# One transposition for the token numbers of each expert, and a later one for the scales

## The chip, the cores and the metric

The kernel runs on one core of a Trainium2 chip. The metric is the device time of one execution in microseconds (us); the times below are those of whole executions, and the profile is of one execution more. The engines are TensorE (PE, with its weight loads as PEld), VectorE (DVE), ScalarE (ACT), GpSimd (POOL) and SyncE (SP), whose queue here issues most transfers. Each engine works through its instructions in the order in which the program lists them.

## What is computed

A gated linear recurrence gives one row of 384 numbers to each of 3072 tokens. A router then picks one of 8 experts for each token, and a second network follows:

```python
logits = x @ w_gate
e_idx = np.argmax(logits, axis=1)
...
gate_w = probs[np.arange(N), e_idx]
eom = 1.0 / (1.0 + np.exp(-(x @ w_output_gate)))
...
    h = np.maximum(x[mask] @ w1[e], 0.0)
    ye = h @ w2[e]
    out[mask] = gate_w[mask, None] * eom[mask, e, None] * ye
...
h = np.maximum(np.maximum(x @ w1, x @ w2), x @ w3)
return (h @ w_out)
```

The factor `gate_w * eom` is one positive number for a token, its scale. The second network lets it through, so the kernel multiplies by it at the very end.

## The kernel before

The recurrence comes first (function `attention`). It writes each token's row with an indirect transfer into the part of the DRAM array `xs` that belongs to its expert. A row there has 385 columns: 384 numbers and, in the last, the token's own number. The experts are ranked by how many tokens they got, and rank e has room for `CAPS[e]` tokens (480, 444, 428, 412, 400, 392, 380, 372).

Then come the experts (function `experts`), 8 of 8 steps each, numbered s = 8e + f. In a step TensorE executes `up(e, f)`, one block of nine matmuls of 128 hidden units for all tokens of the expert (tile `php`), and `down` of the step before, nine matmuls that add into three accumulators (`pacc`). Each product is made of three matmuls (lines 715 to 717) over numbers split in a high and a low part. After `up`, ScalarE makes the high part `hh` (L731) and VectorE the low part `hl` (L732), which the next step's `down` reads. At the last step of an expert the accumulators are copied into `yT` (L746 on ScalarE, L748 on VectorE).

What else a step does is in a table: `at(s, f, ...)` lists a function under a step, and `step(s)` calls the functions of that step after the matmuls, in the order in which they were listed. This order is written out by hand for every engine (`tc.manual_schedule(engines=None)`), so nothing overtakes. The functions that matter here:

- `load_x(e + 1)` in step 8e + 1 fetches the next expert's tokens into `xe`, of which there is one buffer. `transpose_x(e + 1)` in step 8e + 4 turns them (TensorE, `pxt`) and splits them (`xh`, `xl`).
- `numbers(e)` in step 8e (step 1 for e = 0) takes the last column of `xe`, the tokens' numbers, and turns it into lines. TensorE transposes the equal blocks together and the shorter rest by itself, both into the PSUM tile `pid`, and VectorE copies each out (`lines`, `rest`).
- `offset(e)` in step 8e + 5 writes the lines to `ids_d` in DRAM, at a place that a register holds: a transfer for `lines`, and one for `rest`.
- `gates` in step 6 computes all scales on VectorE and ScalarE (`sc`), transposes them on TensorE (`psc`), copies them (`sr`) and sends them to `scale_d` from GpSimd's queue.
- `divide(n)` splits a weight array: `wh` on ScalarE (L156), `wl` mostly on GpSimd (L159). `narrow` (L651 to L653) and `finish` (L659, L660) convert the second network's weights in steps 4j + 2 and 4j + 3.

PSUM has four buffers for `php`, `pxt`, `pid` and `psc` together, taken in turn, and four for `pacc`.

The last stage works through the tokens in the order of `ids_d`: it loads those numbers (L875), fetches the scales by them, and scatters the rows of the result.

Of the kernel before, what the change touches and what calls it, by code (L numbers as in the profile page):

```python
# [10 lines left out]
F32 = mybir.dt.float32  # L11
# [9 lines left out]
B, H, S, D = 4, 8, 768, 48  # L21
HD = H * D
C = 128
NC = S // C
# [4 lines left out]
CAPS = [480, 444, 428, 412, 400, 392, 380, 372]  # L29
# [123 lines left out]
def split(nc, hi, lo, src, hi_eng=None, lo_eng=None):  # L153

    if hi_eng is None:
        nc.scalar.copy(hi, src)  # L156
    else:
        hi_eng.tensor_copy(hi, src)
    (lo_eng or nc.vector).tensor_tensor(out=lo, in0=src, in1=hi.bitcast(F32), op=ALU.subtract)  # L159
# [427 lines left out]
def experts(ctx, tc, io, xs, R, ids_d, scale_d, V32):  # L587

    nc = tc.nc
# [4 lines left out]
    kp = ctx.enter_context(tc.tile_pool(name="kp", bufs=1))  # L594
    yT = kp.tile([128, 3, TP], F32, name="yT")
    LEAST = [e * NT // E for e in range(E)]
    idn = R["idn"]
# [65 lines left out]
        n, i, view = NARROW[j]  # L663
        nc.sync.dma_start(view(V32[n], i), single.pop(j)[0])

    X, RAWX = {}, {}

    def places_of(e):

        if e == 0:  # L670
            n = CAPS[0] // 4
            return [(r * n, n, n) for r in range(4)]
        last = CAPS[e] - 384
        return [(r * 128, 128, min(128, CAPS[e] - r * 128)) for r in range(3)] + ([(384, last, last)] if last > 0 else [])

    def load_x(e):
# [9 lines left out]
                (nc.scalar if k == 1 else nc.sync).dma_start(x[:n, :, ks], src[:, ks].rearrange("(r p) n -> p r n", r=4))  # L686
        X[e] = x

    def numbers(e):

        p = pq.tile([128, 512], F32, tag="pq", name="pid")
        blocks = places_of(e)
        same = [b for b in blocks if b[2] == blocks[0][2]]
        n = same[0][2]
        t = [kp.tile([4, 128], F32, tag="lines", name="lines", bufs=1), kp.tile([1, 128], F32, tag="rest", name="rest", bufs=1)]
        lines = [(0, len(same), n)] + [(len(same) + i, 1, m) for i, (_, _, m) in enumerate(blocks[len(same):])]
        for i, (r, k, m) in enumerate(lines):
            nc.tensor.transpose(p[:k, i * 128:i * 128 + m], RAWX[e][:m, r:r + k, HD], idn[:m, :m])
            nc.vector.tensor_copy(t[i][:k, :m], p[:k, i * 128:i * 128 + m])
        R["lines", e] = t, [(blocks[r][0], k, m) for r, k, m in lines]  # L700

    def transpose_x(e):
        n = CAPS[e]
        hi = xp.tile([128, 3, CAP], F32R, tag="xh", name="xh")[:, :, :n]
        lo = xp.tile([128, 3, CAP], F32R, tag="xl", name="xl")[:, :, :n]
        for k in range(3):
            p = pq.tile([128, 512], F32, tag="pq", name="pxt")
            for r, (r0, _, m) in enumerate(places_of(e)):
                nc.tensor.transpose(p[:, r0:r0 + m], X[e][:m, r, k * 128:(k + 1) * 128], idn[:m, :m])  # L709
            split(nc, hi[:, k], lo[:, k], p[:, :n])  # L710
        RAWX[e], X[e] = X[e], (hi, lo)

    def three(out, st_, mv, start, stop):
        (sh, sl), (mh, ml) = st_, mv
# [50 lines left out]
    def offset(e):  # L765
        R["off"][e] = nc.values_load(R["oi"][0:1, e:e + 1], engines=[ENG.DVE, ENG.Activation, ENG.SP], min_val=LEAST[e], max_val=min(NT, sum(CAPS[:e])),
                                     skip_runtime_bounds_check_because="a sum of counts")
        to = ids_d[bass.ds(R["off"][e], CAPS[e])]
        t, lines = R["lines", e]
        for i, (r0, k, m) in enumerate(lines):  # L770
            nc.sync.dma_start(to[r0:r0 + k * m].rearrange("(r p) o -> r (p o)", r=k), t[i][:k, :m])

    def gates():

        T = B * NC
        lg, oh = R["lg"], R["oh"]
        dl = lg
        nc.vector.tensor_tensor(out=dl[:, :, :E], in0=lg[:, :, :E], in1=R["mx"].unsqueeze(2).to_broadcast([128, T, E]), op=ALU.subtract)
        nc.vector.tensor_tensor(out=dl[:, :, E:], in0=lg[:, :, E:], in1=oh, op=ALU.mult)
        s2 = kp.tile([128, 2, T], F32, name="s2")  # L780
        nc.scalar.activation(out=dl[:, :, :E], in_=dl[:, :, :E], func=AF.Exp)
        nc.vector.tensor_reduce(out=s2[:, 1], in_=dl[:, :, E:], axis=AX.X, op=ALU.add)
        nc.scalar.activation(out=s2[:, 1], in_=s2[:, 1], func=AF.Exp, scale=-1.0)
        nc.vector.tensor_reduce(out=s2[:, 0], in_=dl[:, :, :E], axis=AX.X, op=ALU.add)
        nc.vector.tensor_scalar(out=s2[:, 1], in0=s2[:, 1], scalar1=1.0, scalar2=None, op0=ALU.add)
        nc.vector.scalar_tensor_tensor(out=s2[:, 0], in0=s2[:, 0], scalar=1e-9, in1=s2[:, 1], op0=ALU.add, op1=ALU.mult)
        sc = kp.tile([128, T], F32, name="sc")
        nc.vector.reciprocal(sc, s2[:, 0])
        p = pq.tile([128, 512], F32, tag="pq", name="psc")
        nc.tensor.transpose(p[:T, :128], sc, idn)  # L790
        sr = kp.tile([T, 128], F32, name="sr")
        nc.vector.tensor_copy(sr, p[:T, :128])
        nc.gpsimd.dma_start(scale_d.rearrange("(t p) o -> t (p o)", p=128), sr)
# [4 lines left out]
    def at(s, f, *args):  # L798
        todo.setdefault(max(s, 0), []).append(lambda: f(*args))
# [23 lines left out]
    divide(0, nc.vector)  # L823
    keep_warm(nc, pq.tile([128, 512], F32, tag="pq", name="idle"), idn.bitcast(BF16), WARM[1])
    transpose_x(0)
    divide(1, nc.gpsimd)
    for n in range(2, N1 + N2):
        s = n - 3 if n < N1 else N1 - 19 + (n - N1) * 3 // 2
        at(s, divide, n, nc.vector if n == 2 or n > N1 and n % 2 else nc.gpsimd)
        if n >= 4:  # L830
            at(s - 3, bring, n)
    at(3, offsets)
    at(6, gates)
    for k in range(3):
        at(4 + 3 * k, nc.gpsimd.memset, yT[:, k, CAP:], 0.0)
    for e in range(E):
        at(8 * e or 1, numbers, e)
        at(8 * e + 5, offset, e)
        if e + 1 < E:
            at(8 * e + 1, load_x, e + 1)  # L840
            at(8 * e + 4, transpose_x, e + 1)
# [312 lines left out]
def build(ctx, tc, io):  # L1154
# [26 lines left out]
    for e in range(E):  # L1181
        nc.gpsimd.memset(R["ec"][:, 0, e:e + 1], float(e))
    attention(tc, io["a"], io["qk"], io["v"], io, xs, R)
    experts(tc, io, xs, R, ids_d, scale_d, V32)
    flag = nc.values_load(R["flag"][0:1, 0:1], min_val=0, max_val=128, skip_runtime_bounds_check_because="a count of partitions")
    with tc.If(flag > 0):
# [71 lines left out]
```

## Time and profile before

| | |
|---|---|
| time, median of 3 executions | 831.02 us (830.90 to 832.41) |
| profiled execution | 836.34 us, of which the span from first to last instruction is 834.6 us |
| TensorE matmuls busy | 794.7 us, 95% of the span |
| TensorE weight loads busy | 711.3 us, 85% |
| VectorE busy | 475.8 us, 57% |
| ScalarE busy | 385.6 us, 46% |
| GpSimd busy | 272.5 us, 33% |
| mean granted clock of TensorE | 0.98 |

Matmuls are pipelined, so the start of one to the start of the next is what one costs, not its listed duration. The granted clock is the share of full speed that TensorE got in a stretch: it has two levels, 2.4 GHz (1.00) and 1.2 GHz (0.50), and a value between is a mean of both. A wait is idle time of an engine ahead of an instruction, with the instruction that ended it.

### The profile page before, as it was taken

To read this page: it belongs to the slowest core of one execution; us is meant where nothing else is said; L and a number is where in the kernel's file an instruction comes from. 1 tells how busy PE (TensorE), PEld (TensorE's weight loads), DVE (VectorE), ACT (ScalarE), POOL (GpSimd) and SP (SyncE) were. 2 spreads that over 40 slices of the span, in tenths; PEclk is the share of its full clock that TensorE was granted. 3 is DMA by queue.
4 is the path that set the end of the run, shared out by engine and by line. 5 is a ranking of instruction groups with operands and counts; after the bars stand their busy time and mean duration, and the time that the engine had idled before them with its cause. 6 is when DMAs were issued, how large, how long until landed. Compare 5 with 4: busy or idle time off the path is not lost.

```text
span 834.6 us, 13739 instructions
## 1 busy us (share of the span) xinstructions
PE 794.7 (95%) x5164; PEld 711.3 (85%) x5164; DVE 475.8 (57%) x931; ACT 385.6 (46%) x640; POOL 272.5 (33%) x254
## 2 busy tenths in 40 slices
PE   8889999999996989999999899999999999999995
PEld 6678888888895878898999899888888888888995
DVE  3679998998753555576576643334334343334531
ACT  7779999997641434344444454221212112111221
POOL 1022323323222457445455576031211313021301
PEclk9989999999998999999999899999999999999998
DMA  8974425322213746556656665002012021020200
GB/s 273 269 208 156 159 79 174 112 83 84 83 55 84 260 133 226 185 170 199 224 178 208 208 211 170 1 1 75 20 57 95 1 95 33 26 95 0 96 20 22
DMA packets 61633, 100.78 MB, mean 121 GB/s; under 512 B 7138, under 2 KB 44921, under 8 KB 60537
## 3 DMA queue, kind: packets, MB, share of 16 engines
q1 hardware_dynamic: 57162, 90.11, 34.5%
q0 software_dynamic: 3904, 9.49, 3.1%
q8 instruction: 42, 0.69, 0.4%
q10 hardware_dynamic: 495, 0.25, 0.1%
q14 instruction: 30, 0.25, 0.1%
HBM read 79.64 MB, written 20.15 MB: 120 GB/s over the span
## 4 chain that ended last, share of the span: by engine, by line
PE 55%; DVE 6%; issue 5%; ACT 1%; POOL 1%; DMA 1%; SPq 0%; DVEq 0%; POOLq 0%; ACTq 0%
PE pqt L716 8%; PE pqt L717 8%; PE pqt L715 8%; PE php L715 4%; PE php L716 4%; PE php L717 4%; PE pacc L716 3%; PE pacc L715 3%; PE pacc L717 3%; PE pot L717 3%; PE pot L715 3%; PE pot L716 3%; PE pxt L709 2%; DVE w L653 1%; DVE w L660 1%
## 5 line engine op out<-in xcount | busy, mean ns | idle before, releaser
L159 POOL TENSOR_TENSOR wl<-wraw,wh 128x768 fp32r<-128x768 f32 x68 | 132.8, 1959 | 112.0 <-ACT wh L156 81.1
L717 PE MATMUL pqt<-gh,wl 128*128 128x512 f32 (+1 forms) x378 | 136.1, 360 | 0.0
L716 PE MATMUL pqt<-gl,wh 128*128 128x512 f32 (+1 forms) x378 | 136.0, 360 | 0.0
L715 PE MATMUL pqt<-gh,wh 128*128 128x512 f32 (+1 forms) x378 | 135.7, 359 | 0.0
L156 ACT CAST hh<-h 128x512 fp32r<-128x512 f32 (+1 forms) x42 | 23.5, 560 | 151.2 <-DVE h L905 151.2
L904 DVE TENSOR_TENSOR h<-h,pqt 128x512 f32<-128x512 f32 (+1 forms) x42 | 25.7, 612 | 110.6 <-PE pqt L717 110.6
L731 ACT ACTIVATE hh<-php 128x480 fp32r<-128x480 f32 (+7 forms) x64 | 33.1, 516 | 118.7 <-PE php L717 118.7
L732 DVE SCALAR_TENSOR_TENSOR hl<-php,hh 128x480 fp32r<-128x480 f32 (+7 forms) x64 | 37.4, 584 | 80.3 <-ACT hh L731 80.3
L717 PEld LDWEIGHTS pqt<-gh,wl 128*128 128x128 f32 x378 | 71.3, 189 | 10.6
L716 PEld LDWEIGHTS pqt<-gl,wh 128*128 128x128 f32 x378 | 71.3, 189 | 10.0
L715 PEld LDWEIGHTS pqt<-gh,wh 128*128 128x128 f32 x378 | 71.3, 189 | 9.9
L715 PE MATMUL php<-xh,wh 128*128 128x480 f32 (+7 forms) x192 | 70.2, 366 | 0.0
L716 PE MATMUL php<-xl,wh 128*128 128x480 f32 (+7 forms) x192 | 68.7, 358 | 0.0
L717 PE MATMUL php<-xh,wl 128*128 128x480 f32 (+7 forms) x192 | 68.5, 357 | 0.0
L715 PE MATMUL pacc<-hh,wh 128*128 128x480 f32 (+7 forms) x192 | 67.7, 352 | 0.0
L716 PE MATMUL pacc<-hl,wh 128*128 128x480 f32 (+7 forms) x192 | 67.6, 352 | 0.0
L717 PE MATMUL pacc<-hh,wl 128*128 128x480 f32 (+7 forms) x192 | 67.5, 351 | 0.0
L509 POOL TENSOR_TENSOR run<-run,oh 128x8 bf16<-128x8 bf16 x24 | 13.5, 565 | 161.8 <-DVE oh L486 128.5
L156 ACT CAST wh<-wraw 128x768 fp32r<-128x768 f32 x76 | 61.8, 828 | 9.7 <-DMA wraw<-w 9.3
L903 ACT COPY h<-pqt 128x512 f32<-128x512 f32 (+1 forms) x42 | 22.1, 526 | 88.2 <-PE pqt L717 88.2
L931 POOL DMA_INDIRECT out<-orow,ic x24 | 24.0, 1001 | 117.0 <-ACT orow L930 111.9
L411 PE MATMUL pt<-qT,kT 96*128 96x128 f32 x384 | 51.9, 281 | 2.1 <-DVE qT L212 2.1
(165 smaller groups left out, 1808.8 us busy)
## 6 DMA issues: line engine op xcount, KB each, us to landing
wraw<-w SPq DMA_DIRECT2D x64, 384.0 KB
fa<-a SPq DMA_DIRECT2D x8, 1152.0 KB
a<-a SPq DMA_DIRECT2D x11, 768.0 KB
qk<-qk SPq DMA_DIRECT2D x11, 768.0 KB
raw<-v SPq DMA_DIRECT2D x9, 768.0 KB
xs<-fill SPq DMA_DIRECT2D x8, 721.9 KB
v<-v SPq DMA_DIRECT2D x11, 512.0 KB
xe<-xs SPq DMA_DIRECT2D x21, 192.5 KB
```

The source lines that it names most:

```text
L156: nc.scalar.copy(hi, src)
L159: (lo_eng or nc.vector).tensor_tensor(out=lo, in0=src, in1=hi.bitcast(F32), op=ALU.subtract)
L411: eng.matmul(p[:, z * 128:(z + 1) * 128], lhsT=d["kT", j][:, h], rhs=d["qT", j][:, h], start=True, stop=True)
L709: nc.tensor.transpose(p[:, r0:r0 + m], X[e][:m, r, k * 128:(k + 1) * 128], idn[:m, :m])
L715: nc.tensor.matmul(out, lhsT=sh, rhs=mh, start=start, stop=False)
L716: nc.tensor.matmul(out, lhsT=sh, rhs=ml, start=False, stop=False)
L717: nc.tensor.matmul(out, lhsT=sl, rhs=mh, start=False, stop=stop)
L731: nc.scalar.activation(out=hi, in_=p, func=AF.Relu)
L732: nc.vector.scalar_tensor_tensor(out=lo, in0=p, scalar=0.0, in1=hi.bitcast(F32), op0=ALU.max, op1=ALU.subtract)
L903: nc.scalar.copy(h, pp[0])
L904: nc.vector.tensor_tensor(out=h, in0=h, in1=pp[1], op=ALU.max)
L931: i = nc.gpsimd.indirect_dma_start(out=io["out"], out_offset=bass.IndirectOffsetOnAxis(ap=R["ic", n][:, :1], axis=0), in_=o, in_offset=Non ...
```

## The change

The numbers no longer go through TensorE from `xe`. `numbers(e)` is called at the end of `transpose_x(e)`, and copies the last column of each block of `xe` into a column of a small tile `ln` (128 x 4) on GpSimd. A new function `turn(e)` in step 8e + 2 transposes `ln` as a whole and copies it to `lines`. `offset(e)` writes four lines of equal length in one transfer; what lies beyond an expert's tokens in it is written over by the next expert's. `gates` ends with the reciprocal, and its transposition, copy and transfer are a new function `scales` in step 11.

```diff
-    X, RAWX = {}, {}
+    X = {}
...
+    ln = kp.tile([128, 4], F32, name="ln")
+    lines = kp.tile([4, 128], F32, name="lines")
+    nc.vector.memset(ln, float(1 << 20))
+
     def numbers(e):
 
+        blocks = places_of(e)
+        for r, (_, n, _) in enumerate(blocks):
+            nc.gpsimd.tensor_copy(ln[:n, r:r + 1], X[e][:n, r, HD:])
+
+    def turn(e):
+
         p = pq.tile([128, 512], F32, tag="pq", name="pid")
-        blocks = places_of(e)
-        same = [b for b in blocks if b[2] == blocks[0][2]]
-        n = same[0][2]
-        t = [kp.tile([4, 128], F32, tag="lines", name="lines", bufs=1), kp.tile([1, 128], F32, tag="rest", name="rest", bufs=1)]
-        lines = [(0, len(same), n)] + [(len(same) + i, 1, m) for i, (_, _, m) in enumerate(blocks[len(same):])]
-        for i, (r, k, m) in enumerate(lines):
-            nc.tensor.transpose(p[:k, i * 128:i * 128 + m], RAWX[e][:m, r:r + k, HD], idn[:m, :m])
-            nc.vector.tensor_copy(t[i][:k, :m], p[:k, i * 128:i * 128 + m])
-        R["lines", e] = t, [(blocks[r][0], k, m) for r, k, m in lines]
+        nc.tensor.transpose(p[:4, :128], ln, idn)
+        nc.vector.tensor_copy(lines, p[:4, :128])
...
-        RAWX[e], X[e] = X[e], (hi, lo)
+        numbers(e)
+        X[e] = (hi, lo)
...
-        to = ids_d[bass.ds(R["off"][e], CAPS[e])]
-        t, lines = R["lines", e]
-        for i, (r0, k, m) in enumerate(lines):
-            nc.sync.dma_start(to[r0:r0 + k * m].rearrange("(r p) o -> r (p o)", r=k), t[i][:k, :m])
+        n = places_of(e)[0][1]
+        nc.sync.dma_start(ids_d[bass.ds(R["off"][e], 4 * n)].rearrange("(r p) o -> r (p o)", r=4), lines[:, :n])
...
         nc.vector.reciprocal(sc, s2[:, 0])
+        R["sc"] = sc
+
+    def scales():
+        T = B * NC
         p = pq.tile([128, 512], F32, tag="pq", name="psc")
-        nc.tensor.transpose(p[:T, :128], sc, idn)
+        nc.tensor.transpose(p[:T, :128], R["sc"], idn)
...
+    at(11, scales)
...
-        at(8 * e or 1, numbers, e)
+        at(8 * e + 2, turn, e)
```

On VectorE, the stretch from expert 0's last block to the fourth block of expert 1 (steps 7 to 11; `w` with a number is the array that `narrow` and `finish` make, `yT` the expert's result). Before:

```order
L732 SCALAR_TENSOR_TENSOR hl<-php,hh 128x444
L748 COPY yT<-pacc 128x480 x2
L699 COPY lines<-pid 3x128
L699 COPY rest<-pid 1x60
L732 SCALAR_TENSOR_TENSOR hl<-php,hh 128x444 x2
L652 TENSOR_SCALAR w_4069<-raw 128x768
L653 SCALAR_TENSOR_TENSOR w_4069<-raw,w_4069 128x768
L732 SCALAR_TENSOR_TENSOR hl<-php,hh 128x444
L659 SCALAR_TENSOR_TENSOR w_4069<-raw,w_4069 128x768
```

With the change (lines are numbered anew):

```order
L736 SCALAR_TENSOR_TENSOR hl<-php,hh 128x444
L752 COPY yT<-pacc 128x480 x2
L736 SCALAR_TENSOR_TENSOR hl<-php,hh 128x444 x2
L703 COPY lines<-pid 4x128
L652 TENSOR_SCALAR w_4069<-raw 128x768
L653 SCALAR_TENSOR_TENSOR w_4069<-raw,w_4069 128x768
L736 SCALAR_TENSOR_TENSOR hl<-php,hh 128x444
L798 COPY sr<-psc 24x128
L659 SCALAR_TENSOR_TENSOR w_4069<-raw,w_4069 128x768
```

The copies of the numbers were two, behind the copies of the result and ahead of the second block's `hl`; now there is one, behind the third block's `hl`. The copy of the scales has come in behind the fourth block's.

On TensorE, the start of expert 1, between the last product of expert 0 and its second block. Before:

```order
L716 MATMUL pacc<-hl,wh 128x480
L717 MATMUL pacc<-hh,wl 128x480
L698 MATMUL pid<-idn,xe 3x128
L698 MATMUL pid<-idn,xe 1x60
L715 MATMUL php<-xh,wh 128x444
```

With the change, the place where the transposition now stands, after two more blocks and their products (step 10):

```order
L720 MATMUL pacc<-hl,wh 128x444
L721 MATMUL pacc<-hh,wl 128x444
L702 MATMUL pid<-idn,ln 4x128
L719 MATMUL php<-xh,wh 128x444
L720 MATMUL php<-xl,wh 128x444
```

Two transpositions of parts of `xe` have become one of `ln`, and expert 1's second block follows directly on the last product of expert 0.

On GpSimd, the end of the recurrence and the first steps of the experts (`run` counts tokens, `yT` is cleared behind the first expert's room). Before:

```order
L509 TENSOR_TENSOR run<-run,oh 128x8
L159 TENSOR_TENSOR wl<-wraw,wh 128x768 x6
L799 MEMSET yT 128x2828
L159 TENSOR_TENSOR wl<-wraw,wh 128x768 x2
L793 DMA scale_d<-sr 24x128
```

With the change:

```order
L509 TENSOR_TENSOR run<-run,oh 128x8
L697 COPY ln<-xe 120x1 x4
L159 TENSOR_TENSOR wl<-wraw,wh 128x768 x6
L805 MEMSET yT 128x2828
L697 COPY ln<-xe 128x1 x3
L697 COPY ln<-xe 60x1
L159 TENSOR_TENSOR wl<-wraw,wh 128x768 x3
```

The copies into `ln` stand among the weights' low parts, the first four ahead of all of them, and the transfer of the scales has moved behind five more of these.

## Rows read from the trace of the kernel before

**Rows 1.** The page's first line.

```profile
span 834.6 us, 13739 instructions
```

**Rows 2.** Waits, all engines: who waited for whom, us, times, longest us.

```profile
PEld pid L698 <- DVE lines L699: 13.0, 7, 3.6
...
PE pid L698 <- DVE lines L699: 10.3, 7, 3.2
...
PE psc L790 <- DVE sc L788: 3.1, 1, 3.1
```

**Rows 3.** Timeline of TensorE, start of expert 1: start, us, what, idle before and releaser.

```profile
315.03 0.38 PE L717 MATMUL pacc<-hh,wl 128*128 128x480 f32 x1
...
315.25 0.27 PE L698 MATMUL pid<-idn,xe 128*3 128x128 f32 x1
...
316.34 0.08 PEld L698 LDWEIGHTS pid<-idn,xe 60*1 60x1 f32 x1 [1.23 <-DVE lines L699]
...
316.79 0.36 PE L716 MATMUL php<-xl,wh 128*128 128x444 f32 x1
```

**Rows 4.** Timeline of VectorE, the same place.

```profile
316.02 0.27 DVE L699 COPY lines<-pid 3x128 f32<-3x128 f32 x1
```

**Rows 5.** Timeline of TensorE, start of expert 6.

```profile
467.54 0.34 PE L717 MATMUL pacc<-hh,wl 128*128 128x392 f32 x1
...
471.19 0.37 PE L698 MATMUL pid<-idn,xe 124*1 124x124 f32 x1 [3.20 <-DVE lines L699]
...
476.75 0.40 PE L717 MATMUL pacc<-hh,wl 128*128 128x380 f32 x1
```

**Rows 6.** Timeline of TensorE, steps 6 and 7 of expert 0.

```profile
302.46 0.38 PE L717 MATMUL pacc<-hh,wl 128*128 128x480 f32 x1
...
305.90 0.27 PE L790 MATMUL psc<-idn,sc 128*24 128x128 f32 x1 [3.06 <-DVE sc L788]
...
309.74 0.38 PE L716 MATMUL pacc<-hl,wh 128*128 128x480 f32 x1
...
311.26 0.38 PE L717 MATMUL pacc<-hh,wl 128*128 128x480 f32 x1
```

**Rows 7.** Stretches, TensorE: stretch, length, busy (matmuls), granted clock, DMA share, GB/s.

```profile
300.00:310.00 10.00, 6.94 (x27) 0.83 0.28 82
...
340.00:350.00 10.00, 9.02 (x47) 1.00 0.44 135
470.00:480.00 10.00, 8.81 (x37) 0.66 0.53 156
```

**Rows 8.** Timeline of TensorE, around expert 0's transposition of its numbers.

```profile
280.67 0.38 PE L717 MATMUL pacc<-hh,wl 128*128 128x480 f32 x1
...
281.22 0.38 PE L716 MATMUL php<-xl,wh 128*128 128x480 f32 x1
```

**Rows 9.** Timeline of VectorE, start of expert 6.

```profile
469.46 0.55 DVE L732 SCALAR_TENSOR_TENSOR hl<-php,hh 128x380 fp32r<-128x380 f32 x1
```

**Rows 10.** Timeline of VectorE, from the scales to the first `hl` of expert 1.

```profile
305.45 0.30 DVE L788 RECIPROCAL sc<-s 128x24 f32<-128x24 f32 x1
...
306.41 0.54 DVE L652 TENSOR_SCALAR w<-raw 128x768 int32<-128x768 int32 x1
306.99 0.96 DVE L653 SCALAR_TENSOR_TENSOR w<-raw,w 128x768 int32<-128x768 int32 x1
...
314.30 0.61 DVE L732 SCALAR_TENSOR_TENSOR hl<-php,hh 128x444 fp32r<-128x444 f32 x1
```

**Rows 11.** Timeline of TensorE and of VectorE, steps 34 and 35 (expert 4).

```profile
415.96 0.34 PE L715 MATMUL pacc<-hh,wh 128*128 128x400 f32 x1
...
417.77 2.48 DVE L653 SCALAR_TENSOR_TENSOR w<-raw,w 128x768 int32<-128x768 int32 x1
```

**Rows 12.** Line 500 on GpSimd: min/median/max ns, first and last start, form.

```profile
L500 POOL COPY x<-ids x24: 173/202/1552, 9.6 to 259.3; 128x1 f32<-128x1 f32 x24
```

**Rows 13.** Waits of SyncE's queue, columns as in rows 2.

```profile
SPq L771 <- DMA ids_d<-lines: 19.2, 7, 3.7
```

## Prediction

> **What bounds the kernel now.** I read the views in this order: the page's engine shares, the list of waits, the granted clock by stretches, and then the order of time around each wait. TensorE works through nearly the whole span of 834.6 us [rows 1], so only what it waits for, or executes at the lower clock, can be taken out of the time. In the list of waits two lines of TensorE belong to what the diff touches [rows 2]: the transposition `pid` waits 7 times for `lines`, 10.3 us in all (13.0 us by its weight loads, which stop earlier than the matmuls), and `psc` waits once for `sc`, 3.1 us. No other line of TensorE waits in the experts' stage once the first tokens are there.
>
> The start of expert 1 shows the first kind [rows 3, 4]. TensorE ends the last product of expert 0, does the transposition of the three equal blocks, and then stands still: the second one, of the remaining 60 tokens, writes the same PSUM tile, so it is held until VectorE has copied `lines` out. VectorE comes to that copy late, since it first moves expert 0's result out of PSUM. Nothing that TensorE does next needs the numbers.
>
> The second kind is in step 6 [rows 6]: `psc` transposes the scales in the step that computes them, and TensorE stands until VectorE's chain ends with the reciprocal at 305.75 [rows 10]. After it the matmuls run at the lower clock: the mean granted clock is 0.83 in the stretch with this stop and 0.66 in the one behind expert 6's stop of 3.5 us, but 1.00 in one with a stop of 1.3 us [rows 7].
>
> **What the change takes away.** An ordinary matmul of 480 columns starts 0.217 us after the one before: seven intervals from 309.74 to 311.26 [rows 6]. I scale this by the columns, 0.201 us at 444, 0.181 at 400, 0.172 at 380.
> - Seven boundaries (experts 1 to 7). At expert 1, 1.76 us lie between the last product and the second of the next block, where two intervals would be 0.42: 1.34 us lost, 0.11 more than the weight load's wait of 1.23 [rows 3]. Over seven that makes 13.0 to 13.0 + 7 x 0.11 = 13.8 us [rows 2]; I take 13.5.
> - The clock behind expert 6's stop. From 467.54 to 476.75, 9.21 us, stand 18 intervals worth 3.1 us [rows 5]. Of the 6.1 lost, 3.5 are in the 13.5 already; 2.6 are the clock.
> - The scales. From 302.46 to 309.74, 7.28 us, stand 11 intervals worth 2.4 [rows 6]: 4.9 us lost, 3.3 in the stop and 1.6 at the low clock.
>
> Sum: 13.5 + 2.6 + 4.9 = 21.0 us.
>
> The clock terms, 4.2 us together, are read from one execution. The Trainium skill, in "TensorE: Matmul & The Clock Gate", Part 1, says that the number of slow matmuls after a cold start differs from run to run (6, 11 or 14 in one kernel); this trace has about 10 and 17. By the page's 6 to 14 the two drops would cost about 2.0 to 4.6 us, an estimate with the loss of one matmul here, and the sum would be 18.8 to 21.4.
>
> **What it adds and moves.**
> - Nine transpositions now stand alone in TensorE's queue, eight of `ln` in steps 8e+2 and that of the scales in step 11. The one of expert 0, which waited for nothing, shows their price: 0.55 us where two intervals are 0.43, so 0.12 [rows 8]. One such was there already, so 8 x 0.12 = 0.9 us are added. Their inputs are old by then: `ln` was filled six steps earlier, `sc` five.
> - GpSimd gets four one-column copies for each expert (three for the last two). A like copy of 128x1 takes 0.20 us, 1.55 at worst [rows 12]: 0.8 us on an engine that TensorE waits for nowhere in this stage. The first four stand ahead of `wl` of the second weights, but wait for the same tokens as TensorE's first transpositions and are done while those run. The later ones delay each following `wl` by under 1 us (6 at the worst row), and weights are divided three steps, some 9 us, ahead. I take nothing; if that cover were gone, 0.8 us for each of 7 experts, 5.6.
> - VectorE loses 15 small copies and gets 8 and a fill of `ln`, which runs while it waits for the first weights. Its copy of `lines` now stands behind `hl` of the third block and ahead of `narrow`, and waits there for TensorE. At expert 4 TensorE begins down(4,1) at 415.96 [rows 11], and nine intervals end it at 417.6; the copy would end near 418.3, so L652 and L653 come about 1.1 us later. L653 ended at 420.25, would end at 421.4, and the next `hl` at 421.9. TensorE wants it one transposition, three blocks of nine and one matmul after 417.6, at 422.8. The margin is 0.9 us: nothing lost, but this is the thin place.
> - SyncE loses seven transfers, and with them 19.2 us in which its queue stood for the one before [rows 13]. The weights behind them leave earlier; TensorE waits for no transfer in this stage, so nothing is gained. The transfer of the scales, later by five steps on GpSimd's queue, is read only in the last stage.
> - The load of the next tokens no longer waits for `pid` to read `xe`, but for copies made five steps before: no later than now.
>
> Two stalls stay in part. At expert 6 VectorE is late with the arrays of step 47 (L659, L660): `hl` of the first block starts at 469.46 and takes 0.55 [rows 9]. TensorE, no longer held, has up(6,1) behind it at 469.3 and the first matmul of down(6,0) at 469.4; it would wait some 0.6 us. After step 6 the chain for the scales still occupies VectorE to 305.75; behind it come L652 and L653, `hl`, L659, L660 and the first `hl` of expert 1, 6.2 us by their durations in this trace (six operations, the first at 306.41, the last at 314.30 [rows 10]), so 312.0 if L659 is not stretched, 313.5 if it is. TensorE, never stopped, would want it at 302.7 + five blocks of nine + one matmul = 312.4. So 0 to 1.1 us; I take 0.5.
>
> **The sum.** 21.0 - 0.9 - 1.1 = 19.0 us. The profiled execution took 836.3 us and would take 817.3. The median of the timed runs is 831.0, 5.3 lower; taking the same 19.0 from it gives 812.0 us.
>
> **Rivals.**
> - *The wait changes its name.* VectorE is as busy at each boundary as before, so TensorE may meet it again at `hl` or at the accumulator one block later. For it: the thin margins. Against it: at six of seven boundaries the stop was at most 2.0 us, and a block of 1.5 to 2 us now lies between. If 0.9 us stay at each of 7, 6.3 instead of 1.1: 817.2 us.
> - *The clock terms are the profiled run's own.* It was 5.3 us slower than the timed runs, and the two drops make 4.2 of such a difference. Without them 831.0 - 14.8 = 816.2 us.
> - *Slower: VectorE, held at the new copy, makes TensorE wait for the fourth block's `hl`.* The ground for it is in rows: L653 takes 0.96 us alone [rows 10] and 2.48 where `wl` runs beside it [rows 11]. Two more such stretches of 1.5 in a step, less the margin of 0.9, are 2.1 us for each of six experts (0 to 5, where `narrow` is in that step), 12.6; with a clock drop of 1.6 to 2.6 behind each, 22 to 28, more than the 19.0: 834 to 840 us. It decides from about 2 us of lateness on. Against it: the shift of 1.1 us must push VectorE's operations onto `wl`, not off it, every time. The Trainium skill ("SBUF — State Buffer", "SBUF: two separate sides") calls the port pair that the two engines share an exclusive lock for a whole instruction; the two durations of L653 agree.
> - *It does not take.* TensorE could wait for GpSimd's copies of `ln`; GpSimd would have to lag six steps, some 18 us. Then the time stays near 831.
>
> **Chances and range.** Forecast 0.60, the wait moved on 0.14, no clock terms 0.16, no effect 0.02, slower 0.03; 0.05 for a gain above all of them. The lower end: 21.0 - 0.9 with no stall left is 810.9, less 2 us for the spread of the runs, 809. The upper end: 816.2 and 817.2 with the spread, 819. A measurement of this kernel tells 0.2%, 1.7 us, from no change: faster 0.95, within it 0.02, slower 0.03.
>
> **What would show it.** Right: no line `pid` and no line `psc` in TensorE's waits, a granted clock of 1.00 from 300 to 310 and through expert 6, SyncE without its wait between the numbers' transfers, and at expert 6 a wait of about half a microsecond for `hl`. Wrong: a new line `pacc` or `php` behind `hl` with more than 3 us in all, a clock that falls at another stop, or GpSimd's `ln` named as a releaser.

## The result, and the profile after

| | before | after |
|---|---|---|
| time, medians of one comparison (4 executions each) | 831.71 us (830.90 to 833.28) | 819.40 us (817.71 to 819.58) |
| ratio, with its 95% interval | | 0.9845 (0.9824 to 0.9866) |
| profiled execution | 836.34 us, span 834.6 | 819.29 us, span 817.4 |
| first to last `hh` of the experts' stage, in the profiled executions | 277.2 to 521.6, 244.4 us | 275.5 to 501.8, 226.3 us |
| first to last maximum of the last stage (L905, now L912) | 530.89 to 822.51, 291.6 us | 511.20 to 805.37, 294.2 us |

The change makes the kernel faster by 12.3 us, where 19.0 were forecast. The 819.4 lie 0.4 us above the range; by the ratio, 831.02 would become 818.1, inside it. Between the two profiled executions the span fell by 17.2 us: 18.1 in the experts' stage, 1.7 because its first `hh` came earlier, less 2.55 that the last stage took longer. (That `hh` starts between 273.7 and 278.6 in the profiles of all kernels below, with and without the change, so the 1.7 are no part of it.) The 6.7 us of the miss have two causes, told below: part of the 18.1 us is time at the low clock that other executions of the kernel before don't have, and the last stage, in which no instruction was changed, slowed down.

The waits of TensorE after the change (who waited for whom, us, times, longest us):

```profile
PE pxt L712 <- DMA xe<-xs: 4.5, 2, 4.3
PE pt L411 <- DVE qT L212: 3.5, 1, 3.5
...
PE pacc L720 <- DVE hl L736: 0.4, 1, 0.4
```

No `pid` and no `psc` is left of [rows 2]. `pt` is in the recurrence and the 4.3 us of `pxt` are the first tokens' load; what remains among the experts is one wait for `hl` and one of 0.3 us for `xe`. SyncE's 19.2 us between the numbers' transfers [rows 13] are gone as well: `ids_d<-lines` stands among its waits once, with 2.0 us, in the last stage. The stretches that answer to [rows 7] (stretch, length, busy of TensorE, weight loads, VectorE, ScalarE, GpSimd, granted clock, DMA share, GB/s):

```profile
300.00:310.00 10.00, 10.00 (x49) 8.87 (x48) 9.80 (x16) 4.80 (x9) 6.62 (x4) 1.00 0.23 78
...
454.00:484.00 30.00, 29.01 (x169) 27.92 (x168) 17.15 (x22) 17.21 (x30) 24.64 (x16) 1.00 0.70 221
```

TensorE is busy from 300 to 310 without a break and at 2.4 GHz, where it was busy for 6.94 us at a mean clock of 0.83. The timeline of TensorE in step 10 shows the new transposition; it answers to [rows 3]:

```profile
315.57 0.37 PE L721 MATMUL pacc<-hh,wl 128*128 128x444 f32 x1
315.78 0.28 PE L702 MATMUL pid<-idn,ln 128*4 128x128 f32 x1
315.81 0.45 PE L719 MATMUL php<-xh,wh 128*128 128x444 f32 x1
316.10 0.36 PE L720 MATMUL php<-xl,wh 128*128 128x444 f32 x1
```

From the last product to the second of the next block 0.53 us pass, where two intervals of 0.20 would be 0.40: it costs 0.13 us and waits for nothing. The one stop that is left, at the first block of expert 6:

```profile
455.48 0.33 PE L719 MATMUL pacc<-hh,wh 128*128 128x380 f32 x1
456.25 0.44 PE L720 MATMUL pacc<-hl,wh 128*128 128x380 f32 x1 [0.43 <-DVE hl L736]
```

That is 0.77 us where an interval is 0.17: 0.60 lost. GpSimd's new copies, by the view of the tile `ln` (min/median/max ns, first and last start), are short:

```profile
L697 POOL COPY ln<-xe x30: 173/180/919, 272.2 to 470.4; 128x1 f32<-128x1 f32 x21, 120x1 f32<-120x1 f32 x4, 60x1 f32<-60x1 f32 x1, 44x1 f32<-44x1 f32 x1
```

The last stage is the surprise. Each of its steps ends with a maximum on VectorE; the third and the thirtieth over 512 tokens lie 27 steps apart, the third and the last over 256 tokens 9. Before:

```profile
545.28 0.69 DVE L905 TENSOR_TENSOR h<-h,pqt 128x512 f32<-128x512 f32 x1 [1.28 <-PE pqt L717]
...
768.82 0.69 DVE L905 TENSOR_TENSOR h<-h,pqt 128x512 f32<-128x512 f32 x1 [1.28 <-PE pqt L717]
...
783.74 0.42 DVE L905 TENSOR_TENSOR h<-h,pqt 128x256 f32<-128x256 f32 x1 [0.24 <-PE pqt L717]
...
822.51 0.42 DVE L905 TENSOR_TENSOR h<-h,pqt 128x256 f32<-128x256 f32 x1 [0.59 <-PE pqt L717]
```

After:

```profile
525.88 0.69 DVE L912 TENSOR_TENSOR h<-h,pqt 128x512 f32<-128x512 f32 x1 [1.34 <-PE pqt L721]
...
752.50 0.69 DVE L912 TENSOR_TENSOR h<-h,pqt 128x512 f32<-128x512 f32 x1 [1.34 <-PE pqt L721]
...
767.20 0.42 DVE L912 TENSOR_TENSOR h<-h,pqt 128x256 f32<-128x256 f32 x1 [0.56 <-PE pqt L721]
...
805.37 0.42 DVE L912 TENSOR_TENSOR h<-h,pqt 128x256 f32<-128x256 f32 x1 [0.56 <-PE pqt L721]
```

A step over 512 tokens took 223.54 / 27 = 8.279 us and now takes 226.62 / 27 = 8.393; one over 256 took 38.77 / 9 = 4.308 and now takes 38.17 / 9 = 4.241. Thirty steps of the one kind and twelve of the other give 30 x 0.114 - 12 x 0.067 = 2.6 us more. TensorE waits for nothing there in either kernel.

### The profile page after: what moved, and what is told of

It is laid out like the page before. It is cut to its first block, busy times and chain, and to the rows that moved or that the text cites. A ratio compares the mean times of both kernels' runs of the same rounds, so it can differ in the third digit from the quotient of the medians.

```text
span 817.4 us, 13700 instructions
## 1 busy us (share of the span) xinstructions
PE 790.0 (97%) x5157; PEld 703.8 (86%) x5157; DVE 472.7 (58%) x925; ACT 385.6 (47%) x640; POOL 278.2 (34%) x284
## 4 chain that ended last, share of the span: by engine, by line
PE 59%; issue 5%; DMA 1%; DVE 1%; POOL 1%; SPq 0%; ACT 0%; DVEq 0%; POOLq 0%; ACTq 0%
PE pqt L719 8%; PE pqt L721 8%; PE pqt L720 8%; PE php L719 4%; PE php L720 4%; PE php L721 4%; PE pacc L720 4%; PE pacc L721 4%; PE pacc L719 4%; PE pot L720 3%; PE pot L719 3%; PE pot L721 3%; PE pxt L712 2%; DMA xe<-xs 1%; POOL out L938 0%
```

## The experiments

The first four ran beside one series of the kernel before (median 834.9 us), the next four beside another (833.73), the last four beside a third (831.66). Ratios are to the series that ran beside; across the three, compare ratios and not times.

**x1, the same addresses as before.** `lines` and `rest` took 512 bytes a partition each; `ln` takes 32 (its four numbers are 16, rounded up) and the new `lines` 512. So every tile that is placed behind them, those of the last stage among them, moved by 480 bytes. The edit gives `ln` the room of 512:

```diff
-    ln = kp.tile([128, 4], F32, name="ln")
+    ln = kp.tile([128, 128], F32, name="ln")[:, :4]
```

> The changed kernel with ln made as wide as the tile rest was (128 columns of which 4 are used), so that every tile behind it lies at the address that it had before; nothing else differs. In the trace of the changed kernel a step of the last stage over 512 tokens takes 8.38 us, in that of before 8.27 (30 such steps), and one over 256 takes 4.21 against 4.27 (12). Theory A, the address of what TensorE reads sets its pace: 8.27 and 4.27 again, and 2.6 us less than the changed kernel, some 816.8. Rival, the two executions differ by chance: 8.38 stays or varies from run to run, 819.4.

Measured: 822.51 us, ratio 0.9857 (0.9827 to 0.9886). The steps of the last stage are back at 8.279 and 4.309 us, 291.62 from first to last: the addresses made the 2.55 us. The kernel is not faster for it (the changed kernel has 0.9845), since two stops, of 1.5 and 0.6 us, appeared at expert 1. The longer one, on TensorE:

```profile
326.57 0.47 PE L720 MATMUL pacc<-hl,wh 128*128 128x444 f32 x1 [1.49 <-DVE hl L736]
```

VectorE ahead of it:

```profile
319.39 0.28 DVE L703 COPY lines<-pid 4x128 f32<-4x128 f32 x1 [0.72 <-PE pid L702]
319.60 3.88 DVE L652 TENSOR_SCALAR w<-raw 128x768 int32<-128x768 int32 x1
323.51 2.47 DVE L653 SCALAR_TENSOR_TENSOR w<-raw,w 128x768 int32<-128x768 int32 x1
325.90 0.61 DVE L736 SCALAR_TENSOR_TENSOR hl<-php,hh 128x444 fp32r<-128x444 f32 x1
```

and GpSimd beside it:

```profile
318.81 1.86 POOL L159 TENSOR_TENSOR wl<-wraw,wh 128x768 fp32r<-128x768 f32 x1 [1.71 <-ACT wh L156]
320.61 2.46 POOL L805 MEMSET yT<- 128x2828 f32 x1
323.02 2.14 POOL L159 TENSOR_TENSOR wl<-wraw,wh 128x768 fp32r<-128x768 f32 x1
```

This is the prediction's thin place. The copy held VectorE until 319.6; L652, which takes 0.54 us by itself [rows 10], ended 0.41 us after GpSimd's fill of `yT` did, and L653 0.82 us after the next `wl`. TensorE, at `down` of the block, waited for the `hl` behind them. In the kernel after, VectorE asked a microsecond before the fill, while another `wl` ran; L652 ended 0.42 us behind that `wl`, and L653 took its 0.96 us beside the fill. VectorE, and GpSimd under it:

```profile
316.30 1.48 DVE L652 TENSOR_SCALAR w<-raw 128x768 int32<-128x768 int32 x1
317.81 0.96 DVE L653 SCALAR_TENSOR_TENSOR w<-raw,w 128x768 int32<-128x768 int32 x1
```

```profile
315.51 1.85 POOL L159 TENSOR_TENSOR wl<-wraw,wh 128x768 fp32r<-128x768 f32 x1 [1.70 <-ACT wh L156]
317.30 2.89 POOL L805 MEMSET yT<- 128x2828 f32 x1
```

Here the fill pays: 2.89 us instead of 2.46, the 0.4 of L652. The Trainium skill ("SBUF — State Buffer", "SBUF: two separate sides") says that whichever of the two engines starts first gets the shared ports for its whole instruction; of VectorE's operations it counts those in a two-port mode and, only against a GpSimd operation that reads SBUF, those with two SBUF inputs. On the whole instruction these rows agree, in both directions, and so does L653 with its two inputs: 0.96 us beside the fill, which reads nothing, and 2.47 beside `wl`.

Which of the two goes first, the rows do not settle. L652 is listed 1.00 us ahead of the fill in the kernel after and 1.01 us ahead in x1, both times while a `wl` ran, and it went first in the one and second in the other. x3, with the same wide `ln`, repeats x1; x5 repeats the kernel after. What decides stays open.

**x2, the kernel before, shifted.** A tile of 32 bytes ahead of `lines`, which nothing uses but a fill:

```diff
+    gap = kp.tile([128, 8], F32, name="gap")
+    nc.vector.memset(gap, 0.0)
```

> The kernel before with one tile of 32 bytes more (filled once) ahead of the tiles that TensorE reads in the last stage, which moves them by 32 bytes; they then start at a multiple of 512 bytes, as in the changed kernel. Theory A: 8.38 us for a step over 512 tokens and about 2.6 us slower than before, some 834. Rival, chance: as before, 831.5, and 8.27.

Measured: 838.29 us, ratio 1.0048 (1.0028 to 1.0069), slower by 2.3 to 5.8 us with nothing else changed. The maxima of the same two steps over 512 tokens:

```profile
544.84 0.69 DVE L907 TENSOR_TENSOR h<-h,pqt 128x512 f32<-128x512 f32 x1 [1.34 <-PE pqt L719]
...
771.46 0.69 DVE L907 TENSOR_TENSOR h<-h,pqt 128x512 f32<-128x512 f32 x1 [1.34 <-PE pqt L719]
```

226.62 / 27 = 8.393 us, and 4.241 over 256 tokens: to the nanosecond the pace of the changed kernel, though that one moved by -480 bytes and this one by +32, which lie 512 apart.

**x3, the numbers' part alone** (with the room of 512 bytes): the diff without `scales`, so that `psc` stays in step 6.

```diff
-        at(8 * e or 1, numbers, e)
+        at(8 * e + 2, turn, e)
...
```

> The numbers' part alone, with ln at full width so that addresses are those of before: the scales stay in step 6. Theory B, the two drops of the clock are rare in the timed runs: 13.5 less 0.9 for the transpositions and 0.6 for the stop left at expert 6, so 12.0 below before, 819.5. Rival, the drops are in most runs: 2.6 more, 816.9. In the trace no wait at pid, still 3 us at psc.

Measured: 826.81 us, ratio 0.9913 (0.9883 to 0.9944), 5 to 10 us gained and not the 12.0 expected. `pid` waits no more; `psc` does, 3.1 us, in this profile with a clock of 1.00 behind it. The stop at expert 1 is there too, 1.6 us for `hl`; that expert takes 33.21 us where it takes 31.15 without the stop (x6), which is 2.1 of what is missing.

**x4, the scales' part alone**, with the old `numbers`:

```diff
+    at(11, scales)
```

> The scales' part alone, addresses as before: psc in step 11, numbers as before. Theory B: 3.3 us less 0.1 for the transposition, 828.3. Rival, the clock drops in most runs: 1.6 more, 826.7. Rival, the stop moves to the next hl: no gain, 831.5.

Measured: 833.20 us, ratio 0.9977 (0.9959 to 0.9996), 0.3 to 3.4 us gained. From the first `hh` of expert 0 to that of expert 1 the profile has 31.53 us where the kernel before had 36.39, the 4.9 us of the prediction. But expert 1 took 35.17 instead of 32.26. The stretch behind its stop for `pid`:

```profile
310.00:320.00 10.00, 8.00 (x33) 6.80 (x32) 4.66 (x8) 3.06 (x5) 5.85 (x4) 0.83 0.73 243
```

In the kernel before the clock was 1.00 there, and 0.83 in the ten microseconds ahead. With one stop taken out, the low clock came behind the next one. The halves together (x1) gain 9.5 to 14 us, their single gains sum to about 9.

**x5, the changed kernel once more**, beside the next three.

> The changed kernel itself, once more, on the chip of the experiments and in the same call as the three below. Theory (its gain is the stops taken out, less 2.5 us for the last stage's changed pace): the steps over 512 tokens again 8.39 us and those over 256 again 4.24, no pid and no psc in TensorE's waits, 4 us or less lost to stops among the experts; 818 to 821 us, ratio to before 0.980 to 0.986. Rival (the pace of the last stage was that one execution's own): 8.28 and 4.31, and 815 to 818 us. A stop of over 1 us at expert 1, as the padded kernel had, would say that VectorE's collision there falls one way or the other from run to run and does not come from the pad.

Measured: 820.25 us, ratio 0.9844 (0.9827 to 0.9861). The steps are 8.393 and 4.241 us again, the wait for `hl` at expert 6 0.4 again, the experts' stage 226.4 us. The stop at expert 1 did not appear. The two profiles with the wide `ln` and the fill in step 10 (x1, x3) have it, the two with the narrow one don't: it belongs to the kernel and not to the profiled run by chance, as far as four profiles tell.

**x6, the fills of `yT` elsewhere.** x1's kernel with

```diff
-        at(4 + 3 * k, nc.gpsimd.memset, yT[:, k, CAP:], 0.0)
+        at(5 + 4 * k, nc.gpsimd.memset, yT[:, k, CAP:], 0.0)
```

> The padded changed kernel with GpSimd's three fills of yT moved from steps 4, 7 and 10 to 5, 9 and 13, in which VectorE has no array of the last stage's weights to convert. Theory (TensorE's stop at expert 1 in the padded kernel, 1.66 us and the clock drop behind it, comes from the fill in step 10, which stretches L652 and L653 behind the copy of lines): no stop over 0.7 us at expert 1, that expert near 31.3 us instead of 33.5, the last stage at 8.28 and 4.31, so 818 to 820 us, 2 to 4 less than the padded kernel and 1 to 2 less than the changed one. Rival (the turn in step 10 is late for VectorE whatever GpSimd does): the stop stays, over 1 us, and the time stays near 822.

Measured: 818.67 us, ratio 0.9807 (0.9789 to 0.9825). Expert 1 takes 31.15 us where x1 took 33.53. So the stop at expert 1 needed the fill in step 10. The clock was 1.00 behind it in x1's profile (from 320 to 330): the expectation's clock drop was the second stop, of 0.6 us. Another collision of the same two engines shows instead, at the end of expert 5, with a `wl` as the partner. VectorE, GpSimd and TensorE there, in the timelines of this kernel:

```profile
451.08 2.49 DVE L653 SCALAR_TENSOR_TENSOR w<-raw,w 128x768 int32<-128x768 int32 x1
...
450.82 1.94 POOL L159 TENSOR_TENSOR wl<-wraw,wh 128x768 fp32r<-128x768 f32 x1 [1.07 <-ACT wh L156]
...
454.11 0.45 PE L720 MATMUL pacc<-hl,wh 128*128 128x392 f32 x1 [1.41 <-DVE hl L736]
```

`wl` began 0.26 us before L653 and made it 2.49 us long; in the kernel after, L653 got in first at 450.90 and took 0.96. This stop is not the change's: two of three profiles of the kernel before have it (x11, x12 below).

**x7, the kernel before with a PSUM tile for each transposition.** The line that takes `p` moved into the loop:

```diff
-        p = pq.tile([128, 512], F32, tag="pq", name="pid")
...
         for i, (r, k, m) in enumerate(lines):
+            p = pq.tile([128, 512], F32, tag="pq", name="pid")
```

> The kernel before with one line moved: the remaining block's transposition gets a PSUM tile of its own, so it need not wait until VectorE has copied lines out of the first. Two transpositions, two copies, two transfers, and their step stay as they were; psc stays. Theory (the shared tile makes TensorE wait, not the lateness of the whole step): no pid in TensorE's waits, SyncE still waits between its transfers, psc still 3.1 us; a gain of 8 to 13 us, ratio 0.984 to 0.990. Rival (VectorE is late at each boundary, and TensorE would only meet it one block later): a new line of pacc or php behind hl of 7 us or more, and a gain under 4 us, ratio over 0.995.

Measured: 824.51 us, ratio 0.9879 (0.9858 to 0.9899), 8.4 to 11.8 us gained by one line. TensorE's waits from 280 us to 525:

```profile
PE psc L790 <- DVE sc L788: 3.1, 1, 3.1
PE pxt L709 <- DMA xe<-xs: 1.6, 3, 1.2
PE pacc L716 <- DVE hl L732: 0.2, 1, 0.2
```

So TensorE stood for the shared tile and not for VectorE's lateness, which it does not meet again one block later. Two transpositions and two transfers, with SyncE still waiting 19.0 us between the latter, cost little.

**x8, the turn back in steps 1, 8, 16 and so on**, x1's kernel otherwise:

```diff
-        at(8 * e + 2, turn, e)
+        at(8 * e or 1, turn, e)
```

> The padded changed kernel with the turn of the numbers put back to steps 1, 8, 16 and so on, where before had both transpositions; still one transposition, gathered first, and the scales in step 11. Theory (one transposition, whose tile nobody waits for, takes the stop away wherever it stands; in step 8e+2 it only holds VectorE before L652 and L653): no pid in the waits, the stop of 1.7 us at expert 1 gone since VectorE is not held in step 10, 817 to 820 us. Rival (the two steps' delay is what takes the stop away): TensorE stops again at the boundaries, behind lines or at pacc or php behind hl, over 6 us in all, and 826 to 830 us.

Measured: 819.80 us, ratio 0.9823 (0.9806 to 0.9841). No `pid` waits, and the stop at expert 1 is gone. The two steps' delay is not what takes the stops at `pid` away; in step 10 it only holds VectorE at a worse place. The stop at the end of expert 5 is there as in x6 (1.4 us).

**x9, the next tokens' load earlier**, x6's kernel otherwise:

```diff
-            at(8 * e + 1, load_x, e + 1)
+            at(max(8 * e - 1, 1), load_x, e + 1)
```

> The kernel of x6 (padded, GpSimd's fills of yT in steps 5, 9 and 13) with the load of each next expert's tokens issued two steps earlier, in step 8e-1 instead of 8e+1 (the first one stays in step 1). Theory (TensorE's stops of 0.3 to 1.9 us before the first transposition of expert 7's tokens come from a load that stands on SyncE behind weights waiting for a free buffer): no pxt behind xe after expert 1, and 0.5 to 1.5 us less than the 818.7 of x6: 817 to 818.5, ratio 0.979 to 0.981. Rival (the load waits for its tile, not in the queue): the stop at expert 7 stays over 0.5 us and the time stays at 818.7. The stop of 1.6 us at the end of expert 5 depends on whether GpSimd's wl or VectorE's L653 starts first, and may be there or not.

Measured: 816.01 us, ratio 0.9805 (0.9778 to 0.9833). TensorE's waits from 270 us to 525:

```profile
PE pxt L712 <- DMA xe<-xs: 3.2, 1, 3.2
PE pacc L720 <- DVE hl L736: 2.2, 1, 2.2
```

The 3.2 us are the first tokens'; before expert 7 nothing waits for `xe` any more (1.4 us in x6's profile). So that load stood in SyncE's queue. But a wait of 2.2 us for `hl` came at expert 6's first block, where L659 and L660 stood beside `wl`, in place of x6's 1.4 at the end of expert 5:

```profile
458.15 0.44 PE L720 MATMUL pacc<-hl,wh 128*128 128x380 f32 x1 [2.22 <-DVE hl L736]
```

The profiled execution, 818.92 us, is the slowest of the six, and the ratio is x6's: no gain is shown.

**x10, x9's kernel shifted by 64 bytes:**

```diff
+    kp.tile([128, 16], F32, name="gap")
```

> The kernel of x9 with an unused tile of 64 bytes a partition ahead of lines, so that all tiles of the last stage that lay behind stand 64 bytes further on. Theory (what counts for the pace of the last stage is the place of its tiles against a grid of 64 bytes; the changed kernel moved them by 480, which is 32 off that grid): the steps keep 8.28 us over 512 tokens and 4.31 over 256. Rival (the grid is wider, or any move counts): other lengths, 8.39 and 4.24 or new ones. The time by the one as x9, by the other 2 to 4 us more.

Measured: 815.12 us, ratio 0.9805 (0.9767 to 0.9842). The theory of a grid of 64 bytes falls. The maxima:

```profile
523.18 0.69 DVE L913 TENSOR_TENSOR h<-h,pqt 128x512 f32<-128x512 f32 x1 [1.30 <-PE pqt L722]
...
747.47 0.69 DVE L913 TENSOR_TENSOR h<-h,pqt 128x512 f32<-128x512 f32 x1 [1.30 <-PE pqt L722]
```

224.29 / 27 = 8.307 us, and 4.249 over 256 tokens: a third pair of lengths. Together they make 291.78 us, 0.16 more than x9's, since the one loss and the other gain nearly cancel here.

**x11 and x12, the kernel before, two profiles more.**

> The kernel before, for another profile of it. Theory (the low clock behind psc and behind expert 6's stop differs from one execution to the next, and the profile of before that the prediction was made from had more of it than most): the stops of pid and psc as before, 10 and 3.1 us, but the granted clock from 300 to 310 or through expert 6 (454 to 484) higher than 0.83 and 0.94 in one of the two profiles at least, and the span below 834.6. Rival (the drops belong to the stops): both clocks as before, within 0.03.

> The kernel before once more, a further profile of it; the same expectations as for the run ahead of it.

Measured: 832.64 and 831.47 us, spans 830.9 and 829.7. The stretches of x11, columns as above:

```profile
300.00:310.00 10.00, 6.95 (x26) 5.61 (x25) 6.74 (x13) 3.85 (x7) 2.59 (x3) 0.83 0.26 82
...
454.00:484.00 30.00, 26.89 (x158) 26.17 (x157) 16.67 (x22) 16.65 (x29) 19.77 (x12) 1.00 0.74 237
```

and of x12:

```profile
300.00:310.00 10.00, 6.94 (x34) 5.76 (x33) 7.74 (x14) 3.95 (x7) 3.62 (x3) 1.00 0.27 82
...
454.00:484.00 30.00, 26.77 (x157) 26.05 (x156) 16.77 (x19) 16.53 (x27) 20.12 (x11) 1.00 0.73 235
```

In the profile that the prediction was read from the first stretch had 0.83; the second one had 0.89, not the 0.94 that the expectation gives. x11 has the low clock behind `psc` alone, x12 at neither place, with TensorE idle for as long in all three: 6.94, 6.95 and 6.94 us busy of the first ten. The first and last `hh` of x12 (min/median/max ns, first and last start):

```profile
L731 ACT ACTIVATE hh<-php x64: 480/510/575, 276.3 to 516.7; 128x480 fp32r<-128x480 f32 x8, 128x444 fp32r<-128x444 f32 x8, 128x428 fp32r<-128x428 f32 x8, 128x412 fp32r<-128x412 f32 x8
```

The experts' stage is 240.4 us long there, 241.8 in x11, and was 244.4 in the profile of before. The stop at expert 6 also looked different: 3.2 us at `pid` before, in x12 1.6 us at `hl` in the block of products just ahead and 1.7 at `pid` (1.5 and 1.7 in x11):

```profile
465.43 0.44 PE L716 MATMUL pacc<-hl,wh 128*128 128x392 f32 x1 [1.57 <-DVE hl L732]
466.96 0.27 PE L698 MATMUL pid<-idn,xe 128*2 128x128 f32 x1
468.89 0.27 PE L698 MATMUL pid<-idn,xe 124*1 124x124 f32 x1 [1.66 <-DVE lines L699]
```

The same lateness of VectorE, split in two, and no low clock behind either half.

## Why the prediction was right, and where it was wrong

**Right: what bounds, and the sign.** TensorE's stops at `pid` and at `psc` were real, and no other engine took their place. The rival by which the wait changes its name fell: 0.4 us for `hl` where it asked for 6.3. The rival of no effect fell with GpSimd's copies, 0.18 us each and never a releaser of TensorE.

**Right: the stops' price.** Profile against profile the experts' stage lost 18.1 us, and the forecast for it was 19.0. The scales' part took 36.39 to 31.53 us at expert 0 (x4), 4.86 for the 4.9, the low clock included. The one-line kernel x7 gained 9.2 us by the medians for the `pid` stops alone; what it does not gain of the 13.5 includes, in its profile, a wait of 1.2 us for `xe` ahead of expert 7 and a clock of 0.83 behind it (from 475 to 485), but that profile is the slowest of its four executions, 2.9 us over the median. The added transposition costs 0.13 us for the forecast 0.12, and the rest at expert 6 is 0.60 us for 0.6. The 0.5 us after step 6 did not come.

**Wrong: taking the 19.0 from the median.** The step that failed is the last line of the sum. The two clock terms, 1.6 and 2.6 us, were sized well: between the profile of before and x12, expert 0 differs by 36.39 - 34.85 = 1.5 us and expert 6 by 32.19 - 29.70 = 2.5. But they are not part of every execution. x12 has neither, x11 the first alone, and their times, 831.5 and 832.6 us, lie near the median, while the profiled execution took 836.3. With x2, x3 and x7, which have the stop at `psc` too, the clock fell behind it in four of six profiles. The gain from x12 and x11 to the changed kernel's 226.3 us of the stage is 14.1 and 15.5 us. This was the rival "the clock terms are the profiled run's own", which got 0.16 and had its argument in the text: the profile was 5.3 us over the median, and the two drops made 4.2 of that.

**Wrong: the last stage as it was.** The sum has no term for it; the change was read for what it issues, and not for what it allocates. Moving the tiles by 480 bytes cost 2.55 us. x1 undid it, and x2 made the same loss in the kernel before, without the rest of the change. That 818.1 by the ratio still lies inside the range is luck in part: the range's upper end was set by the rivals and the spread of the runs, not by anything in the last stage.

With both the sum comes out. 831.0 - (13.5 + 3.3) + 0.9 + 0.6 is 815.7, and with 2.55 for the last stage 818.3. The text also held that TensorE waits for no transfer among the experts; the kernel after loses 0.3 us before expert 7 because it arrives earlier than the load (x9 shows where the load stood; x5 loses 0.6). That makes 818.6, where 819.4 was measured; with the first clock term, which some executions have, it would be 817.0, so the agreement is no closer than that.

**Half right: the slower rival.** Its mechanism, VectorE held at the copy of `lines` and then behind GpSimd, exists: x1 and x3 show it at expert 1, 2.4 us by x1 against x6 (33.53 and 31.15). There it needed the fill of `yT` in the same step (x6) and the copy in that step (x8), and it came at one expert, not at six. In the kernel after the same operations stand at the same distance and L652 goes first, for a reason that stays open.

The other waits for `hl` are of another kind, without that copy. At the end of expert 5 L653 stands behind `wl` in x6 and x8, 1.4 us each, and in the kernel before too (x11 1.5, x12 1.6). At expert 6's first block it is L659 or L660, in x9 (2.2), in x10 (0.5) and in the kernel after (0.4, for which the prediction had 0.6). So VectorE's and GpSimd's order there turns with small shifts, and the 1.5 us by which the kernel after is spared the first of these, against x11 and x12, are not shown to be the change's own.

x6 beats both kernels: 0.9807 against 0.9844 of the changed one beside the same series, with intervals that do not meet, if by little (0.9825 and 0.9827). It takes the change, the old addresses, and fills in steps where VectorE has no array to convert.

## What to carry to other kernels

Before a gain is subtracted from a median, see whether its terms belong to the profiled execution or to the kernel: more profiles of the kernel before (x11, x12) show that 4 us of low clock come and go. When an edit adds or drops a tile, list which tiles move, and look at the pace of the stages that read them, also of those that the edit doesn't touch. And a wait on a shared PSUM tile may need only a tile more: x7 got 9.2 us by one line moved where the changed kernel beside the same series (x5) got 13.5.

## What was not expected of the hardware

TensorE's pace depends on where its operands lie in SBUF. One and the same sequence of matmuls took, for a step over 512 and one over 256 tokens, 8.279 and 4.308 us at the old place, 8.393 and 4.241 at +32 bytes and at -480, and 8.307 and 4.249 at +64. If the equal lengths at +32 and -480 are no coincidence, what counts repeats at 512 bytes or at a part of that above 64. The experts' stage shows it too, by less: from expert 2's first `hh` to expert 3's it is 30.10 to 30.11 us in the five kernels with the change at the old place, 30.23 in the changed kernel and in x5, 30.32 in x10. The two lengths move against each other, 1.4% and 1.6% at most. Which operand makes it (the tokens' parts, the products between, or their places against the weights, which did not move), or whether it is the other engines' reads and writes of the tiles that moved, stays open; no run moved them one by one.

The low clock comes behind some stops and not behind others of about the same length. Behind `psc`'s stop of 3.1 us the mean granted clock from 300 to 310 is 0.83, 0.83 and 1.00 in the three profiles of the kernel before, 0.87 in x2, 0.88 in x7 and 1.00 in x3. Behind expert 6's stop it is 0.66 in the profile of before (3.2 us; 470 to 480) and 1.00 in x4 (2.8 us; 465 to 485). It is 0.83 behind shorter ones, of 2.0 us at expert 1 in x4 (310 to 320) and of 2.2 us at expert 6 in x9 (455 to 465).
